# Four weight buffers instead of three, a list that knows what the buffers hold, and a fourth buffer for finished rows

## The chip, the cores and the metric

The kernel runs on one core of a Trainium2 chip. The metric is the device time of one execution in microseconds (us), lower is better. TensorE (PE in the profile) does the matmuls, VectorE (DVE), ScalarE (ACT) and GpSimd (POOL) the rest of the arithmetic, SyncE (SP) issues most DMAs; POOL issues the indirect ones.

## What is computed

There are 14336 tokens of 192 channels. A seven-tap causal filter per head comes first, then two mixtures of experts, each with 8 experts of 192 to 1024 to 192:

```python
x = attn(x, weight)                          # causal filter, taps softmaxed per head
do = x @ w_skip > 0                          # first mixture: only these tokens
e = argmax(x[do] @ w_gate); y = gate * (relu(x @ w1[e]) @ w2[e]); x[do] += y
e2 = argmax(x @ w_gate2 + modality_bias[modality_id])      # second mixture: all tokens
out = gate2 * (relu(x @ w1b[e2]) @ w2b[e2])
```

## The kernel before

Tokens are sorted by expert on the chip and then worked off in blocks ("slots") of 128 rows. A slot is a job: an indirect DMA on POOL gathers the rows (`gather`, tile `gt`), SP transposes them by DMA (`xpose`, tile `xt`, or `xp` for a pair), `mm1` multiplies by the first weight matrix (`w1b`), ACT and DVE split the hidden values into two float16 parts, `mm2` multiplies by the second (`w2b`).

`Ffn.run` writes the 176 jobs out in one fixed order. Jobs 0 to 55 are the first mixture's fixed slots, seven for each expert. Jobs 56 to 61 are its overflow list `l1` (`NS1` = 6 slots for experts with more than 896 tokens). Jobs 62 to 117 are list `lb`: second mixture, the tokens that skipped the first. Jobs 118 to 175 are list `l2`: second mixture, the tokens that the first mixture worked on. In `lb` and `l2` the first 54 and 56 jobs go in pairs that share one set of weights and are multiplied 256 columns at a time; the two last of each list are single.

Which expert a slot belongs to is known only on the chip. `table` writes for each slot the expert and a flag: 1 where this expert differs from the one that last stood in the same buffer. `wload` reads both on SP and issues the load under that flag; a load whose flag is 0 moves nothing. There are three buffers for a pair of weight matrices, taken in turn, so `table` compares with the entry three places earlier (six jobs earlier for pairs); at a list's head it compares with -1, so the first three always load. `wload` is written out as soon as no earlier job still uses the buffer, at most 9 or 10 jobs ahead.

While jobs from 53 on run, `post` takes the first mixture's finished rows in groups of up to four slots: ACT copies them into `h2` (`h` in the profile, three buffers), POOL and DVE complete it, PE and ACT transpose it for the second gate (`xt2`, `xt` in the profile), and SP stores it in `rows2` (line 1153). Three such chains run at a time, handed out in turn by `bg`. ACT, DVE, POOL and PE work strictly in the order written.

The weights of the second mixture are prepared (split in two float16 parts, written to `s1b`, `s2b`) by `lane(1)` in the two tiles `o1` and `o2`, which lie idle after job 53.

Of the kernel before, what the change touches and what calls it, by code (L numbers as in the profile page):

```python
# [12 lines left out]
ALU = mybir.AluOpType  # L13
# [21 lines left out]
XA = 16  # L35
NSEL = 4
LANES = [(0, e) for e in range(E)], [(1, r) for r in range(NSEL)]
RW = 396
# [6 lines left out]
NP2B, NS2B = 27, 56  # L45
NP2A, NS2A = 28, 58
NC1 = NSA + CAP - 1
NR2 = NC1 * 128 + 384
# [67 lines left out]
class Moe:  # L116
# [63 lines left out]

    def plain(self, tmp):
        nc, cp = self.nc, self.cp
        dz = tmp.tile([128, RW], F16, name="rC")
        nc.gpsimd.memset(dz, 0.0)
        nc.gpsimd.memset(f32v(dz.unsqueeze(1))[:, 0, MB + 4:MB + 5], BIGID)
        self.dz = dz
        self.c8 = cp.tile([128, 8], F32, name="c8")
        self.iota(self.c8, [[-1, 8]], base=8)
        self.mt3 = cp.tile([TP, NT, 3], F32, name="mt3")
        nc.gpsimd.memset(self.mt3, 0.0)  # L190
        self.iota(self.mt3[:, :, 1], [[TP, NT]], base=TP - 1, cm=-1)
        self.code = cp.tile([128, 2, NT], F32, name="code")
        nc.gpsimd.memset(self.code, 0.0)
        self.codeA = cp.tile([128, NC1], F32, name="codeA")
        nc.gpsimd.memset(self.codeA, 0.0)
        self.cont = cp.tile([128, 8, GT], F32, name="cont")
        nc.gpsimd.memset(self.cont, 1.0)
        nc.gpsimd.memset(self.cont[:, :, 0:1], 0.0)
        self.iq = cp.tile([128, 128, 8], F16, name="iq")
        self.iota(self.iq, [[1, 128], [0, 8]])  # L200
        self.tri = cp.tile([128, 128], F32, name="tri")
        self.iota(self.tri, [[1, 128]], cm=-1)
        nc.gpsimd.tensor_scalar(self.tri, self.tri, 0.0, None, ALU.is_gt)
        self.val = cp.tile([128, 16], F16, name="val")
        self.iota(self.val, [[1, 16]], base=1, cm=16)
        self.valr = cp.tile([128, 16], F16, name="valr")
        self.iota(self.valr, [[128, 16]], base=1, cm=1)
        self.g2k = cp.tile([128, 9], F32, name="g2k")
        self.iota(self.g2k, [[2048, 9]])

    def tables(self, bias2, wgs, mod, tmp):
        nc, tc, cp = self.nc, self.tc, self.cp
# [43 lines left out]
        nc.gpsimd.tensor_copy(self.modf, mi[:, :, 0])  # L256
        self.bias = cp.tile([TP, NT, 8], F32, name="biasall")
        self.bias_for(nc.gpsimd, self.bias, self.modf, NT, tmp)
# [452 lines left out]

    def table(self, S, np, o, tag, pool, ob, res, lp, top=None):
        nc = self.nc
        en = o[2]
        ef = ob.tile([128, S + 6], F32, name="esl", bufs=1)
        nc.vector.memset(ef[:, 0:6], -1.0)
        for k in range(2 if np else 1):
            ex = pool.tile([128, S, 8], F32, name="rB")
            nc.vector.tensor_tensor(ex, self.iq[:, :S, :], en[:, k].unsqueeze(1).to_broadcast([128, S, 8]), ALU.is_ge)
            yield 1  # L720
            e1 = pool.tile([128, S], F32, name="e1") if k else ef[:, 6:]
            nc.vector.tensor_reduce(e1, ex, AX.X, ALU.add)
            yield 1
        tab = lp.tile([128, S, 2], I32, name="tab" + tag)
        if np:
            nc.vector.tensor_tensor(ef[:, 6:], ef[:, 6:], e1, ALU.add)
            nc.vector.tensor_copy(tab[:, :, 0], ef[:, 6:])
            nc.vector.tensor_scalar(tab[:, :, 0], tab[:, :, 0], 7, None, ALU.bitwise_and)
            nc.vector.tensor_copy(ef[:, 6:], tab[:, :, 0])
        else:  # L730
            nc.vector.tensor_scalar(ef[:, 6:], ef[:, 6:], 7.0, None, ALU.min)
        if top is not None:
            nc.vector.tensor_scalar(ef[:, 6:], ef[:, 6:], float(top), None, ALU.min)
        if top is not None or not np:
            nc.vector.tensor_copy(tab[:, :, 0], ef[:, 6:])
        for a, b, c, d in ((0, 2 * np, 0, 1), (2 * np, min(2 * np + 3, S), 2 * np, 2), (2 * np + 3, S, 2 * np + 6, 1)) if np else ((0, S, 3, 1),):
            if b > a:
                nc.vector.tensor_tensor(tab[:, a:b, 1], ef[:, a + 6:b + 6], ef[:, c:c + d * (b - a - 1) + 1:d], ALU.not_equal)
        res["tab"] = tab
        yield 1  # L740
# [14 lines left out]

    def route(self, code, nst, tag, pool, ob, res, base=0, lag=1, S=None, np=0, lp=None, val=None, perm=False, top=None):
        lp = lp or self.cp
        S = S or nst
        r, o = [], []
        for w in self.ranks(code, pool, 1, r):  # L760
            yield w
        for w in self.slots(r[3], np, perm, pool, o):
            yield w
        self.left(r[3], nst, perm, o, tag, pool, res, lp)
        for w in self.place(r, np, o, pool):
            yield w
        q, sl = self.qsl(o[4], pool)
        yield 1
        for w in self.table(S, np, o, tag, pool, ob, res, lp, top):
            yield w  # L770
        for w in self.invert(S, q, sl, pool, ob, tag, res, lp, lag, base, val):
            yield w
# [229 lines left out]
class Ffn:  # L1002
    def __init__(self, m, ctx, out):
        self.m, self.nc, self.tc, self.out = m, m.nc, m.tc, out
        cp = m.cp
        self.w1b = [cp.tile([128, 4, F], F16, name=f"w1b{i}") for i in range(2)]
        self.w2b = [cp.tile([128, W2C + 2], F16, name=f"w2b{i}") for i in range(2)]
        self.g = ctx.enter_context(m.tc.tile_pool(name="fg", bufs=7))
        self.pairs, self.pw, self.pg = 0, None, None

# [107 lines left out]
    def post(self, x2, mt, nb, va, dst, code):  # L1118
        nc, m, p = self.nc, self.m, self.late
        h2 = p.tile([128, NB1, RW], F16, name="h2", bufs=3)  # L1120
        mo = f32v(h2)[:, :nb, :]
# [55 lines left out]
    def run(self, jobs, bg, pre, fill, need):  # L1177
# [7 lines left out]
        def wload(k, w, m):  # L1185
            if not 0 <= k < n or (k, w) in wl or jobs[k]["s1"] is None or jobs[k]["part"]:
                return
            jb = jobs[k]
            if any(jobs[j]["b"] == jb["b"] for j in range(m, k)):
                return  # L1190
# [109 lines left out]
def build(tc, x, cw, m1w1, m1w2, mod, bias2, m2w1, m2w2, wgs, out):  # L1300
    with ExitStack() as ctx:
# [18 lines left out]
        next(taps)  # L1320
        tables = m.tables(bias2, wgs, mod, rt)
        next(tables)
        for _ in taps:
            pass
        m.consts()
        m.plain(rt)

# [75 lines left out]
        def late_pools():  # L1403
            st.close()
            m.py.append(m.py2)
            m.ph.append(m.ph3)
            px = ctx.enter_context(tc.tile_pool(name="px", bufs=1))
            w["x"] = px.tile([128, NC - XA, D], F32, name="x2s")
            po = sp.enter_context(tc.tile_pool(name="po", bufs=1))
            pw2 = sp.enter_context(tc.tile_pool(name="pw2", bufs=2))  # L1410
            w["pw2"] = pw2
            tkw.add(lane(1))
            o = po.tile([128, 4, F], F16, name="o1"), po.tile([128, W2C + 2], F16, name="o2")
            w["o"] = o
            tk.add(routes())

        def x2of(c, nb):
# [36 lines left out]
        for k in range(NSA - SB + SA, NSA):  # L1454
            jobs[k].update(b=2, s1=s1[0], s2=s2[0], fix=0 if k == NSA - SB + SA else None)
        jobs += [mk(1, l1, j, rows, col=NSA + j, s=0, b=j % 3) for j in range(NS1)]
        for l, nst, np, src, g in ((lb, NS2B, NP2B, rows, NS1), (l2, NS2A, NP2A, rows2, NS1 + NS2B - NP2B)):
            jobs += [mk(2, l, j, src, s=1, b=(g + j // 2) % 3, size=2, part=j % 2) for j in range(2 * np)]
            jobs += [mk(2, l, j, src, s=1, b=(g + j - np) % 3) for j in range(2 * np, nst)]
        n1, n2 = NC, NC + NS2B  # L1460

        def bg(i, pt):
# [9 lines left out]
            if i == n1 - 9 and pt == 4:  # L1472
                tk.drain()
                tkw.drain()
                sp.close()
                ffn.pg = ctx.enter_context(tc.tile_pool(name="pg", bufs=2))
                ffn.pw = pw
                m.ph.pop()
                ffn.late = ctx.enter_context(tc.tile_pool(name="pl", bufs=4))
            if i == n1 - 7 and pt == 0:  # L1480
# [5 lines left out]
            if n1 + 7 < i < n2 - 6 and not tk.live and "idx" not in l2:  # L1486
                tk.add(m.route(m.codeA[:, 0:NC], NS2A, "2", rt, ob, l2, lag=2, np=NP2A, perm=True, top=NSEL - 1))
            if i == n2 and pt == 0:
# [5 lines left out]
            if i == n2 - 6 and pt == 0:  # L1494
                tk.drain()
                if "idx" not in l2:
                    tk.add(m.route(m.codeA[:, 0:NC], NS2A, "2", rt, ob, l2, lag=2, np=NP2A, perm=True, top=NSEL - 1))
                    tk.drain()
# [19 lines left out]
        ffn.rows2 = rows2  # L1518
        ffn.run(jobs, bg, pre, fill, need)
        obr = ctx.enter_context(tc.tile_pool(name="obr", bufs=1))  # L1520
        for n in ("nrem", "un"):
# [61 lines left out]
```

## Time and profile before

| what | value |
|---|---|
| three runs | 1000.71 to 1004.94 us, median 1002.71 |
| profiled execution | 1001.22 us, of which the span from first to last instruction is 999.3 |
| PE busy | 916.0 us, 92% |
| DVE, ACT, POOL busy | 587.8, 476.0, 513.7 us |
| mean granted TensorE clock | 0.968 |
| DMA | 150.79 MB, mean 151 GB/s |

The difference between profiled time and span, 1.9 us, lies outside the first and last instruction. PE's busy share says that it sets the pace; what can be gained is in its idle stretches and in stretches at a lower clock.

### The profile page before, as it was taken

The page shows a single profiled execution, that of the slowest core. Times are in us where ns is not written, and L with a number is a line of the kernel's source. Part 1 is how long each engine was busy: PE and PEld are TensorE (multiplying, and loading weights), DVE is VectorE, ACT ScalarE, POOL GpSimd, SP SyncE. Part 2 cuts the span into 40 slices and gives each one's busy share as a digit, 9 for nine tenths or more (in the row PEclk, how much of TensorE's full clock was granted, in tenths as well). Part 3 has the DMA queues.
Part 4 walks back from the last instruction along what each step waited for, and adds up shares of the span by engine and source line. Part 5 has one row for each costly group of instructions (what it writes and reads, how often), then busy time and mean ns, then how long its engine had stood idle before and what let it go on. Part 6 is the DMA issues. An engine that isn't in the chain of part 4 may idle for free. (4 is left out here: it accounts for less than half of the span.)

```text
span 999.3 us, 28865 instructions
## 1 busy us (share of the span) xinstructions
PE 916.0 (92%) x11000; PEld 852.3 (85%) x11000; DVE 587.8 (59%) x1624; ACT 476.0 (48%) x895; POOL 513.7 (51%) x985
## 2 busy tenths in 40 slices
PE   6999868997999999976999999999989999999993
PEld 4666668987999999976888988999988999999992
DVE  5689977899798877543555465864332333333330
ACT  3877743545686654443645654333333333333430
POOL 4155543742646365562777675454544555555431
PEclk9999859999999999997999999999999999999997
DMA  9595576754868776599333333222492222332240
GB/s 318 192 334 187 186 198 191 197 137 132 237 181 249 214 223 197 163 233 329 91 95 98 109 98 111 70 64 62 135 295 63 73 74 69 74 73 74 74 122 16
DMA packets 106197, 150.79 MB, mean 151 GB/s; under 512 B 80591, under 2 KB 85689, under 8 KB 100800
## 3 DMA queue, kind: packets, MB, share of 16 engines
q1 hardware_dynamic: 91424, 119.34, 38.6%
q0 software_dynamic: 13920, 28.87, 12.1%
q8 instruction: 89, 1.46, 0.6%
q10 hardware_dynamic: 704, 0.63, 0.2%
q14 instruction: 60, 0.49, 0.2%
HBM read 174.22 MB, written 51.08 MB: 225 GB/s over the span
## 5 line engine op out<-in xcount | busy, mean ns | idle before, releaser
L71 PEld LDWEIGHTS <-w1b 128*128 128x128 f16 x4840 | 370.6, 99 | 43.1 <-issue 14.4
L71 DVE SCALAR_TENSOR_TENSOR ws<-bank,ws 128x512 f16<-128x512 f32 x220 | 151.3, 690 | 267.9 <-ACT ws L71 224.4
L71 PE MATMUL bank<-xp,w1b 128*128 128x256 f16 x2200 | 264.6, 274 | 5.2 <-DMA xp<-gt 2.9
L71 PE MATMUL bank<-w2b,ws 128*128 128x192 f16 x2640 | 239.2, 246 | 0.1
L71 PEld LDWEIGHTS <-ws 128*128 128x128 f16 (+2 forms) x2696 | 224.0, 98 | 2.7 <-issue 0.2
L71 POOL DMA_INDIRECT out_dram<-u,si x114 | 115.4, 1012 | 188.0 <-ACT u L71 76.0
L71 ACT ACTIVATE ws<-bank 128x512 f16<-128x512 f32 x220 | 130.6, 597 | 99.5 <-PE bank L71 89.0
L71 PE MATMUL bank<-xt,w1b 128*128 128x128 f16 x2640 | 165.6, 222 | 12.5 <-DVE hlo L71 7.4
L71 ACT ACTIVATE hh<-bank 128x512 f16<-128x512 f32 x132 | 78.5, 594 | 143.6 <-PE bank L71 133.0
L71 PE MATMUL bank<-w2b,hh 128*128 128x192 f16 x1056 | 141.2, 250 | 2.3 <-DMA w2b<-s2a 1.9
L71 PE MATMUL bank<-w2b,hlo 128*128 128x192 f16 x528 | 131.6, 249 | 0.6 <-DVE hlo L71 0.6
L71 ACT ACTIVATE u<-bank,c 128x192 f32<-128x192 f32 x114 | 48.1, 422 | 171.5 <-PE bank L71 148.0
L71 DVE SCALAR_TENSOR_TENSOR hlo<-bank,hh 128x512 f16<-128x512 f32 x132 | 90.0, 685 | 55.2 <-ACT hh L71 49.1
L71 PEld LDWEIGHTS <-hh 128*128 128x128 f16 x1056 | 96.3, 100 | 3.3 <-issue 2.9
L71 POOL DMA_INDIRECT gt<-rows,idxm x62 | 62.7, 1011 | 10.2 <-issue 6.9
L71 POOL TENSOR_TENSOR xs<-gt 128x128 f32<-128x128 f16 x124 | 53.7, 455 | 26.9 <-DVE x2a L71 13.0
L71 POOL DMA_INDIRECT gt<-rows,idx x58 | 57.5, 991 | 9.3 <-issue 6.7
L71 PE MATMUL bank<-xg,band 128*112 128x384 f32 x128 | 57.6, 537 | 1.7 <-DVE hl L71 1.7
L71 ACT COPY xtb<-bank 128x672 f16<-128x672 f16 x64 | 46.0, 720 | 19.2 <-PE bank L71 18.9
L71 PEld LDWEIGHTS <-hlo 128*128 128x128 f16 x528 | 52.4, 99 | 1.0 <-DVE hlo L71 0.8
L71 POOL DMA_INDIRECT gt<-rows,idxs x44 | 47.0, 1069 | 6.7 <-POOL c L71 3.3
L71 POOL TENSOR_SCALAR ef<-ef 128x4 f32<-128x4 f32 (+1 forms) x16 | 4.4, 277 | 86.8 <-DVE ef L71 86.8
(293 smaller groups left out, 1135.1 us busy)
## 6 DMA issues: line engine op xcount, KB each, us to landing
w1b<-s1b SPq DMA_DIRECT2D x59, 1024.0 KB
w2b<-s2b SPq DMA_DIRECT2D x59, 768.5 KB
xg<-in_x_dram SPq DMA_DIRECT2D x7, 1536.0 KB
rows<-hl SPq DMA_DIRECT2D x7, 1386.0 KB
ws<-in_moe_w_dram SPq DMA_DIRECT2D x12, 768.0 KB
s1a<-w1b SPq DMA_DIRECT2D x8, 1024.0 KB
w1b<-s1a SPq DMA_DIRECT2D x7, 1024.0 KB
s2a<-w2b SPq DMA_DIRECT2D x8, 768.5 KB
```

Of the source, the lines that this page charges most:

```text
L71: r = f(*args, **kw)
```

## The change

Overflow slots and second-mixture slots take four buffers in turn, in the order 0, 3, 1, 2. The fourth is made of `o1` and `o2`, whose pool now stays open, and joins the list at job 53. `table` therefore compares four entries back (eight jobs for pairs). For `l2`, the four entries ahead of the list's head are no longer -1 but the experts that the last four weight sets of `lb` left in the buffers (`held`, four copies on DVE). `h2` gets four buffers. To make room, three tables of phase 1 (`mt3`, `cont`, `biasall`) move into a pool that is closed after phase 1, and the pool of the `post` tiles is closed after the last job and made anew with one `h2` buffer for the rarely needed loop behind it. The diff, cut to its core (`ef[:, 6:]` becomes `ef[:, 8:]` throughout `table`; `held` is passed through `route`):

```diff
+RING = (0, 3, 1, 2)
+NR2B = NS2B - NP2B
-        self.mt3 = cp.tile([TP, NT, 3], F32, name="mt3")
+        self.mt3 = st.tile([TP, NT, 3], F32, name="mt3", bufs=1)
-        self.cont = cp.tile([128, 8, GT], F32, name="cont")
+        self.cont = st.tile([128, 8, GT], F32, name="cont", bufs=1)
-        self.bias = cp.tile([TP, NT, 8], F32, name="biasall")
+        self.bias = st.tile([TP, NT, 8], F32, name="biasall", bufs=1)
...
-        ef = ob.tile([128, S + 6], F32, name="esl", bufs=1)
-        nc.vector.memset(ef[:, 0:6], -1.0)
+        ef = ob.tile([128, S + 8], F32, name="esl", bufs=1)
+        nc.vector.memset(ef[:, 0:8], -1.0)
+        for k, v in enumerate(held or ()):
+            nc.vector.tensor_copy(ef[:, 2 * k:2 * k + 1], v)
...
-        h2 = p.tile([128, NB1, RW], F16, name="h2", bufs=3)
+        h2 = p.tile([128, NB1, RW], F16, name="h2", bufs=self.nh)
...
-            if any(jobs[j]["b"] == jb["b"] for j in range(m, k)):
+            if jb["b"] >= len(self.w1b) or any(jobs[j]["b"] == jb["b"] for j in range(m, k)):
...
-            po = sp.enter_context(tc.tile_pool(name="po", bufs=1))
+            po = ctx.enter_context(tc.tile_pool(name="po", bufs=1))
...
+        def held():
+            return [lb["tab"][:, 2 * r if r < NP2B else r + NP2B, 0:1] for r in range(NR2B - 4, NR2B)]
...
-        jobs += [mk(1, l1, j, rows, col=NSA + j, s=0, b=j % 3) for j in range(NS1)]
+        jobs += [mk(1, l1, j, rows, col=NSA + j, s=0, b=RING[j % 4]) for j in range(NS1)]
-            jobs += [mk(2, l, j, src, s=1, b=(g + j // 2) % 3, size=2, part=j % 2) for j in range(2 * np)]
+            jobs += [mk(2, l, j, src, s=1, b=RING[(g + j // 2) % 4], size=2, part=j % 2) for j in range(2 * np)]
...
                 sp.close()
+                ffn.w1b.append(w["o"][0])
+                ffn.w2b.append(w["o"][1])
-                ffn.late = ctx.enter_context(tc.tile_pool(name="pl", bufs=4))
+                ffn.late = sp.enter_context(tc.tile_pool(name="pl", bufs=4))
...
         ffn.run(jobs, bg, pre, fill, need)
+        sp.close()
+        ffn.late, ffn.nh = ctx.enter_context(tc.tile_pool(name="plr", bufs=1)), 1
```

## Rows read from the trace of the kernel before

**Rows 1.** The page, part 2: PE's busy tenths, its clock, GB/s, in 40 slices.
```profile
PE   6999868997999999976999999999989999999993
PEclk9999859999999999997999999999999999999997
...
GB/s 318 192 334 187 186 198 191 197 137 132 237 181 249 214 223 197 163 233 329 91 95 98 109 98 111 70 64 62 135 295 63 73 74 69 74 73 74 74 122 16
```
**Rows 2.** Windows: length, busy PE, PEld, DVE, ACT, POOL (instructions), PEclk, DMA share, GB/s.
```profile
401.00:420.00 19.00, 19.00 (x287) 19.00 (x285) 10.40 (x22) 7.37 (x14) 9.59 (x29) 1.00 0.55 149
...
450.00:460.00 10.00, 7.48 (x80) 6.86 (x80) 2.69 (x8) 1.54 (x3) 0.19 (x1) 0.83 1.09 371
460.00:470.00 10.00, 5.54 (x49) 4.84 (x50) 2.29 (x9) 3.38 (x7) 5.21 (x12) 0.66 0.78 313
```
**Rows 3.** Timeline of PE, 430 to 515: start, length, operation, idle time before it, releaser.
```profile
442.07 1.28 PE L71 MATMUL bank<-xt,w1b 128*128 128x128 f16 x20 [2.11 <-DMA xt<-gt]
...
450.06 1.37 PE L71 MATMUL bank<-xt,w1b 128*128 128x128 f16 x20 [2.38 <-DMA xt<-gt]
...
464.46 0.25 PE L71 MATMUL bank<-g,xt 128*128 128x16 f16 x3 [6.92 <-ACT xt L71]
...
464.83 2.34 PE L71 MATMUL bank<-xp,w1b 128*128 128x256 f16 x10
...
469.77 1.25 PE L71 MATMUL bank<-xp,w1b 128*128 128x256 f16 x10
```
**Rows 4.** Waits of PE, whole span: total us, times, longest.
```profile
PE bank L71 <- DMA w2b<-s2a: 1.9, 2, 1.3
```
**Rows 5.** Timeline of ACT, 425 to 485.
```profile
463.19 0.83 ACT L71 CAST h<-x2a 128x768 f16<-128x768 f32 x1 [8.91 <-DMA rows<-h]
...
474.31 0.83 ACT L71 CAST h<-x2s 128x768 f16<-128x768 f32 x1
```
**Rows 6.** Tile `h`: idle time of its engines before its instructions, times.
```profile
  DMA rows<-h: 12.5, 4
```
**Rows 7.** Timeline of SP's queue, 330 to 500.
```profile
401.21 0.36 SPq L1025 DMA_DIRECT2D w1b<-s1a  x1
...
436.01 1.24 SPq L1031 DMA_TRANSPOSE xt<-gt  x1
...
443.69 1.19 SPq L1031 DMA_TRANSPOSE xt<-gt  x1
...
456.51 0.53 SPq L1153 DMA_DIRECT2D rows<-h  x1
```
**Rows 8.** Timeline of SP's queue, 690 to 770.
```profile
711.04 0.72 SPq L1025 DMA_DIRECT2D w1b<-s1b  x1
...
732.21 0.33 SPq L1025 DMA_DIRECT2D w1b<-s1b  x1
734.13 3.60 SPq L1026 DMA_DIRECT2D w2b<-s2b  x2
739.33 0.08 SPq L1025 DMA_DIRECT2D w1b<-s1b  x1
739.51 2.57 SPq L1031 DMA_TRANSPOSE xp<-gt  x2
```
**Rows 9.** Timeline of PE, 700 to 768.
```profile
750.49 3.52 PE L71 MATMUL bank<-xp,w1b 128*128 128x256 f16 x20 [2.86 <-DMA xp<-gt]
...
756.31 2.35 PE L71 MATMUL bank<-xp,w1b 128*128 128x256 f16 x20
...
760.48 2.35 PE L71 MATMUL bank<-xp,w1b 128*128 128x256 f16 x20
```
**Rows 10.** DMA issues, whole span: times issued, KB each (1024 bytes).
```profile
w1b<-s1b SPq DMA_DIRECT2D x59, 1024.0 KB
w2b<-s2b SPq DMA_DIRECT2D x59, 768.5 KB
```
**Rows 11.** Groups of instructions on DVE by form, 600 to 660: busy us, mean ns.
```profile
L71 DVE TENSOR_REDUCE tt<-se 128x1 f32<-128x8 f32 x2 | 0.3, 160 | 0.1
```

More of the change, by code (lines that the diff above doesn't have):

```diff
@@ L179, in consts, with plain @@
         nc.vector.tensor_copy(self.identf, self.ident)
-    def plain(self, tmp):
+    def plain(self, tmp, st):
         nc, cp = self.nc, self.cp
@@ L209, in plain, with tables @@
         self.iota(self.g2k, [[2048, 9]])
-    def tables(self, bias2, wgs, mod, tmp):
+    def tables(self, bias2, wgs, mod, tmp, st):
         nc, tc, cp = self.nc, self.tc, self.cp
@@ L710, in place, with table @@
         o.append(pos)
-    def table(self, S, np, o, tag, pool, ob, res, lp, top=None):
+    def table(self, S, np, o, tag, pool, ob, res, lp, top=None, held=None):
         nc = self.nc
         en = o[2]
-        ef = ob.tile([128, S + 6], F32, name="esl", bufs=1)
-        nc.vector.memset(ef[:, 0:6], -1.0)
+        ef = ob.tile([128, S + 8], F32, name="esl", bufs=1)
+        nc.vector.memset(ef[:, 0:8], -1.0)
+        for k, v in enumerate(held or ()):
+            nc.vector.tensor_copy(ef[:, 2 * k:2 * k + 1], v)
         for k in range(2 if np else 1):
@@ L720, in table @@
             yield 1
-            e1 = pool.tile([128, S], F32, name="e1") if k else ef[:, 6:]
+            e1 = pool.tile([128, S], F32, name="e1") if k else ef[:, 8:]
             nc.vector.tensor_reduce(e1, ex, AX.X, ALU.add)
@@ L725, in table @@
         if np:
-            nc.vector.tensor_tensor(ef[:, 6:], ef[:, 6:], e1, ALU.add)
-            nc.vector.tensor_copy(tab[:, :, 0], ef[:, 6:])
+            nc.vector.tensor_tensor(ef[:, 8:], ef[:, 8:], e1, ALU.add)
+            nc.vector.tensor_copy(tab[:, :, 0], ef[:, 8:])
             nc.vector.tensor_scalar(tab[:, :, 0], tab[:, :, 0], 7, None, ALU.bitwise_and)
-            nc.vector.tensor_copy(ef[:, 6:], tab[:, :, 0])
+            nc.vector.tensor_copy(ef[:, 8:], tab[:, :, 0])
         else:
-            nc.vector.tensor_scalar(ef[:, 6:], ef[:, 6:], 7.0, None, ALU.min)
+            nc.vector.tensor_scalar(ef[:, 8:], ef[:, 8:], 7.0, None, ALU.min)
         if top is not None:
-            nc.vector.tensor_scalar(ef[:, 6:], ef[:, 6:], float(top), None, ALU.min)
+            nc.vector.tensor_scalar(ef[:, 8:], ef[:, 8:], float(top), None, ALU.min)
         if top is not None or not np:
-            nc.vector.tensor_copy(tab[:, :, 0], ef[:, 6:])
-        for a, b, c, d in ((0, 2 * np, 0, 1), (2 * np, min(2 * np + 3, S), 2 * np, 2), (2 * np + 3, S, 2 * np + 6, 1)) if np else ((0, S, 3, 1),):
+            nc.vector.tensor_copy(tab[:, :, 0], ef[:, 8:])
+        for a, b, c, d in ((0, 2 * np, 0, 1), (2 * np, min(2 * np + 4, S), 2 * np, 2), (2 * np + 4, S, 2 * np + 8, 1)) if np else ((0, S, 4, 1),):
             if b > a:
-                nc.vector.tensor_tensor(tab[:, a:b, 1], ef[:, a + 6:b + 6], ef[:, c:c + d * (b - a - 1) + 1:d], ALU.not_equal)
+                nc.vector.tensor_tensor(tab[:, a:b, 1], ef[:, a + 8:b + 8], ef[:, c:c + d * (b - a - 1) + 1:d], ALU.not_equal)
         res["tab"] = tab
@@ L754, in left, with route @@
             res["un"] = un
-    def route(self, code, nst, tag, pool, ob, res, base=0, lag=1, S=None, np=0, lp=None, val=None, perm=False, top=None):
+    def route(self, code, nst, tag, pool, ob, res, base=0, lag=1, S=None, np=0, lp=None, val=None, perm=False, top=None, held=None):
         lp = lp or self.cp
@@ L768, in route @@
         yield 1
-        for w in self.table(S, np, o, tag, pool, ob, res, lp, top):
+        for w in self.table(S, np, o, tag, pool, ob, res, lp, top, held):
             yield w
@@ L1008, in __init__ @@
         self.g = ctx.enter_context(m.tc.tile_pool(name="fg", bufs=7))
-        self.pairs, self.pw, self.pg = 0, None, None
+        self.pairs, self.pw, self.pg, self.nh = 0, None, None, 4
     def gather(self, idx, src):
@@ L1320, in build @@
         next(taps)
-        tables = m.tables(bias2, wgs, mod, rt)
+        tables = m.tables(bias2, wgs, mod, rt, p1.p2)
         next(tables)
@@ L1325, in build @@
         m.consts()
-        m.plain(rt)
+        m.plain(rt, p1.p2)
         step, scaled = [-1], [0]
@@ L1455, in build @@
             jobs[k].update(b=2, s1=s1[0], s2=s2[0], fix=0 if k == NSA - SB + SA else None)
-        jobs += [mk(1, l1, j, rows, col=NSA + j, s=0, b=j % 3) for j in range(NS1)]
-        for l, nst, np, src, g in ((lb, NS2B, NP2B, rows, NS1), (l2, NS2A, NP2A, rows2, NS1 + NS2B - NP2B)):
-            jobs += [mk(2, l, j, src, s=1, b=(g + j // 2) % 3, size=2, part=j % 2) for j in range(2 * np)]
-            jobs += [mk(2, l, j, src, s=1, b=(g + j - np) % 3) for j in range(2 * np, nst)]
+        jobs += [mk(1, l1, j, rows, col=NSA + j, s=0, b=RING[j % 4]) for j in range(NS1)]
+        for l, nst, np, src, g in ((lb, NS2B, NP2B, rows, NS1), (l2, NS2A, NP2A, rows2, NS1 + NR2B)):
+            jobs += [mk(2, l, j, src, s=1, b=RING[(g + j // 2) % 4], size=2, part=j % 2) for j in range(2 * np)]
+            jobs += [mk(2, l, j, src, s=1, b=RING[(g + j - np) % 4]) for j in range(2 * np, nst)]
         n1, n2 = NC, NC + NS2B
@@ L1486, in bg @@
             if n1 + 7 < i < n2 - 6 and not tk.live and "idx" not in l2:
-                tk.add(m.route(m.codeA[:, 0:NC], NS2A, "2", rt, ob, l2, lag=2, np=NP2A, perm=True, top=NSEL - 1))
+                tk.add(m.route(m.codeA[:, 0:NC], NS2A, "2", rt, ob, l2, lag=2, np=NP2A, perm=True, top=NSEL - 1, held=held()))
             if i == n2 and pt == 0:
@@ L1496, in bg @@
                 if "idx" not in l2:
-                    tk.add(m.route(m.codeA[:, 0:NC], NS2A, "2", rt, ob, l2, lag=2, np=NP2A, perm=True, top=NSEL - 1))
+                    tk.add(m.route(m.codeA[:, 0:NC], NS2A, "2", rt, ob, l2, lag=2, np=NP2A, perm=True, top=NSEL - 1, held=held()))
                     tk.drain()
```

## The prediction

> **What bounds the kernel now.** I read the page's table of slices first. PE is at 9 in nearly every slice, so the end is set by PE, and only PE's holes and its slow stretches can give time back. After phase 1 there are two weak places: the two slices from 450 to 500 us (7 and 6) and the slice from 750 to 775 (8) [rows 1]. A slice is 999.3 / 40 = 25 us.
>
> Then I read the windows around the first place. From 450 to 460 PE is busy 7.48 of 10 us at a granted clock of 0.83, from 460 to 470 only 5.54 of 10 at 0.66, while the DMA engines are busy throughout (shares 1.09 and 0.78, 371 and 313 GB/s) [rows 2]. A DMA burst and a PE hole at the same time: either PE itself waits for data, or something that PE needs waits for the burst.
>
> The timeline of PE names the holes. There is 2.11 us ahead of 442.07 and 2.38 us ahead of 450.06, both ended by the landing of a transposed block, and 6.92 us ahead of 464.46, ended by ACT's copy of a transposed group [rows 3]. The list of waits adds 1.9 us in two waits for `w2b` [rows 4]. Sum: 2.1 + 2.4 + 6.9 + 1.9 = 13.3 us.
>
> The longest hole is not ACT's own work. ACT's timeline shows that it sat 8.91 us ahead of one CAST into `h`, waiting for the store `rows<-h` [rows 5]: the fourth group of finished rows wanted the buffer of the first. ACT works in order, so the copy that PE wanted stood behind that CAST. SP issued the store at 456.51 [rows 7]; the buffer came free at 463.19. The store needed 6.7 us because weights were in flight. The tile view counts four such waits, 12.5 us in all [rows 6].
>
> At the second place, SP's queue shows the weights of list `l2` being loaded: between 711.04 and 732.21 four issues of `w1b` take 0.33 us or longer, where an issue that moves nothing takes about 0.08 [rows 8]. A pair of matrices is 1024 + 768.5 KB [rows 10], 1.84 MB; four are 7.3 MB, which agrees with 295 GB/s in the slice from 725 to 750 against 62 to 74 GB/s in quiet ones [rows 1]. The transposes issued at 739.51 are behind them, and PE waits 2.86 us ahead of 750.49 for a transposed block. The pair step that starts there takes 756.31 - 750.49 = 5.8 us, the next one 760.48 - 756.31 = 4.2 [rows 9].
>
> **The first part: `h2` with four buffers.** It takes away the fourth group's wait for the first group's store. Removed: 6.9 us of PE idle time [rows 3], and the slow stretch behind it. The ten matmuls at 464.83 take 2.34 us, ten like them at 469.77 take 1.25 [rows 3]: 1.1 us lost in these alone; for the window as a whole 5.54 x (1 - 0.66) = 1.9 us [rows 2]. I take 1.7. Sum 8.6 us.
>
> What is late next? The fifth group's CAST, which wants the first group's buffer in the new kernel. It follows the fourth's by 474.31 - 463.19 = 11.1 us [rows 5], of which 1.7 were the clock. Without the wait the fourth runs at about 463.2 - 8.9 = 454.3, the fifth at about 454.3 + 9.4 = 463.7, and the first store lands at 463.2. So it arrives with next to nothing in hand. I take off 1.0 us: 7.6 us stay. Bounds: 8.6 if the store is early, 2.6 if the store lands 6 us later relative to the jobs.
>
> **The second part: four buffers in the overflow list.** A pair of matrices at 371 GB/s [rows 2] takes 1.84 / 0.371 = 4.9 us. A single job has 40 matmuls in `mm1` and 24 in `mm2`; from 401 to 420 PE did 287 in 19 us [rows 2], so 64 take 4.2 us. The six overflow slots and the first three pairs need nine loads in a row, so this stretch runs at the pace of the DMA engines. From 401 to 420 they are only at a share of 0.55 and 149 GB/s [rows 2]: there is room ahead of the burst. With three buffers, the load of overflow slot 2 has to wait for buffer 2, which the first mixture's last four jobs hold until about 401 + 4 x 4.2 = 418. With the order 0, 3, 1, 2 it goes into buffer 1, which is free at 401.21, when slot 1's load went there [rows 7]; slot 1's goes to the new buffer at job 54, about 410. Every later load can start one job earlier, about 4 to 5 us. So one load moves from the burst into the room ahead of it. The two waits for `w2b` (slots 2 and 3) go: 1.9 us [rows 4]. The transposes at 436.01 and 443.69 that PE waited for [rows 7] landed 6 us after their issue; each has one `w1b` and one `w2b` in front of it, and this stays so, one job further on. I count nothing for these 4.5 us, with bounds of +6 us (both waits and their slow stretch go; 10 us at 0.83 [rows 2] are 1.7 us) and -6 us (each gets another pair of matrices ahead of it, less what they have in hand).
>
> List `lb` loads its weights into four buffers instead of three: one load more, 4.9 us of DMA time, behind the others and wanted only three pairs later. From 475 on the engines are far from full (the slices behind are at 91 to 111 GB/s [rows 1]); it costs nothing as long as no transpose stands behind it with less than 4.9 us in hand.
>
> **The third part: `l2` knows what the buffers hold.** Nearly all issues in `lb` and `l2` move nothing [rows 1, 8], so both lists are almost wholly one expert, the most loaded one, and the four issues at 711 to 732 must be one for the last single of `lb` (another expert) and three for the head of `l2`, which compares with -1. With `held`, the first three weight sets of `l2` find that expert in their buffers and move nothing; the fourth finds the single's expert and loads, three pairs later. Four loads become two, 2 x 4.9 = 9.8 us less DMA time around 725 to 745, and the transposes of 739.51 find a free queue. That gives back 2.9 us of waiting and 5.8 - 4.2 = 1.6 us of slow clock [rows 9], and some 0.5 us of small waits around it that I leave out: 4.5 us. The four copies on DVE are of the size of the smallest instructions there, 160 ns [rows 11]: 0.64 us in `l2`'s routing around 640 us, where PE is at 9 in every slice [rows 1]. DVE is nearly full there, so it could cost PE up to 0.6 us; I take 0.3.
>
> The tables that change pools issue nothing new. They are last used in phase 1, and what is laid over them is first written much later. Zero, with a bound of 1 us loss for a write that waits for a last reader.
>
> **Sum.** 7.6 + 1.9 + 0 + 4.5 - 0.3 = 13.7 us. From the profiled execution's 1001.2 us that makes 987.5. The median of the three runs is 1.5 us above this execution, so I expect a median of 989.
>
> **The rivals.** *All holes close.* The transposes of the overflow list land in time as well because the burst starts a load earlier: 6 us more, 983. For it speaks the room at 401 to 420; against it that a load stays in front of each.
>
> *The stall is handed on.* With ACT freed, the fifth group waits for the first store, or PE runs into the burst, since nine loads at 4.9 us are 44 us whatever PE does. Then the first part gives only 2.6 us and the time is 989 + 5 = 994. Against it: the engines fall back to 91 GB/s in the slice from 475 [rows 1], so the burst was over by then, and among PE's waits for weights those for the first mixture's second matrices are the only ones of note, 1.9 us [rows 4].
>
> *Slower: weights in front of transposes.* SP has one queue, and what is behind a load waits for it: the store of 456.51 took 6.7 us, the transposes some 6. Four buffers allow four weight sets in flight, and the order in which SP's instructions are written may put two in front of a transpose where there was one. Each costs PE 4.9 us plus the 1.7 us of slow clock, 6.6 us. Two such stalls use up the gain of 13.7, and from three on, 1002.7 - 13.7 + 19.8 = 1009, the kernel is slower by over 0.5%. The Trainium skill ("DMA: Bandwidth & Descriptors", "Queues, rings and completion order") says that SP owns one ring on each DMA engine, and that a ring is consumed in order; it gives the rule behind this case, and the 6.7 us of the store agree with it. Against the case: the overflow stretch has only six single transposes, and the same count of loads is spread over a longer time.
>
> *It doesn't do what it says.* If the copied entries don't match (another expert, or an order of buffers that is off), `l2` loads four sets instead of three and the second place gets worse by up to 4.9 us: 989 + 4.5 + 4.9 = 998.
>
> **Chances.** The forecast, part by part as above, 0.57 (984.5 to 993); all holes close 0.17; handed on 0.14; slower 0.07; doesn't do what it says 0.05. An effect below 0.5%, 5 us, can't be told from none here. Faster by more (below 997.7): 0.57 + 0.17 + 0.11 of the third case = 0.85. Within: 0.03 of the third, 0.05 of the last and 0.01 of the fourth, where only two stalls come, 0.09. Slower: the other 0.06. The range reaches from 981 (all holes close, with 2 us of the small waits) to 997 (handed on, with nothing left of the first part); below and above it lie about 0.05 and 0.13.
>
> **What would show it.** Right: no wait of ACT for `rows<-h` above 1 us and no PE hole ended by ACT's `xt` at 457; clock 1.00 where it was 0.66; no wait for `w2b<-s2a`; a 1 MB load of `w1b` issued right behind the one at 401; two long issues fewer between 711 and 733; no PE wait at 750. Wrong: new PE waits for `xt<-gt` or `xp<-gt` between 420 and 480, a wait of ACT for `rows<-h` at the fifth group, or PE waiting for weights at the first pairs.

## The result and the profile after

| | before | after |
|---|---|---|
| median, six runs each | 999.57 us | 987.14 us |
| lowest to highest | 994.07 to 1004.94 | 984.29 to 989.52 |
| profiled execution, its span | 1001.22, 999.3 | 987.25, 985.4 |
| PE busy in the span | 916.0 us | 913.1 us |
| DMA | 150.79 MB | 148.96 MB |

The ratio is 0.9875, with a 95% interval of 0.9849 to 0.9902: 12.4 us in the medians, 14.0 in the profiled executions. 989 was forecast, with 981 to 997 as the range; the forecast started from 1002.71, the median of the first three runs, and the six runs of the kernel before have 999.57. DMA fell by 1.83 MB, one pair of matrices: one load more in `lb`, two fewer in `l2`.

The page of the changed kernel, part 2, answers to [rows 1]:

```profile
PE   6999859997999999999899999999999999999993
PEclk9999857999999999999999999999999999999997
...
GB/s 320 207 332 188 188 197 192 177 162 71 299 143 262 200 269 149 244 242 344 140 95 109 98 96 114 72 62 65 144 143 72 72 68 75 74 74 74 71 125 15
```

A slice of the changed kernel is 985.4 / 40 = 24.6 us. The weak place from 425 to 475 (7 and 6 before) is down to one 8 (468 to 493), the 8 from 725 to 750 is gone, and the slice in which `l2`'s weights were loaded moves 143 GB/s instead of 295. The windows of the changed kernel (columns as in [rows 2]) show that the weight burst is as dense as before, and that PE is busy through the middle of it; smaller holes are left at 440 and at 470:

```profile
440.00:450.00 10.00, 7.91 (x104) 7.57 (x102) 3.32 (x13) 3.85 (x9) 7.47 (x22) 0.83 1.02 293
450.00:460.00 10.00, 10.00 (x131) 9.59 (x129) 5.95 (x19) 5.58 (x12) 5.26 (x12) 1.00 1.02 340
460.00:470.00 10.00, 8.64 (x104) 7.88 (x103) 6.70 (x16) 6.92 (x17) 6.36 (x15) 1.00 1.03 407
470.00:480.00 10.00, 7.25 (x69) 6.18 (x68) 5.25 (x25) 3.70 (x8) 2.24 (x8) 0.83 0.79 151
```

PE's timeline at the first place, changed kernel:

```profile
441.72 2.29 PE L73 MATMUL bank<-xt,w1b 128*128 128x128 f16 x20 [1.39 <-DMA xt<-gt]
...
448.82 1.28 PE L73 MATMUL bank<-xt,o 128*128 128x128 f16 x20 [0.70 <-DMA xt<-gt]
...
457.92 1.25 PE L73 MATMUL bank<-xp,w1b 128*128 128x256 f16 x10
...
474.47 1.25 PE L73 MATMUL bank<-xp,w1b 128*128 128x256 f16 x10 [2.75 <-DMA xp<-gt]
...
475.82 2.34 PE L73 MATMUL bank<-xp,w1b 128*128 128x256 f16 x10
...
480.78 1.25 PE L73 MATMUL bank<-xp,w1b 128*128 128x256 f16 x10
```

And two rows of the same view of the kernel before, for the third pair's first and third ten matmuls:

```profile
483.41 1.25 PE L71 MATMUL bank<-xp,w1b 128*128 128x256 f16 x10
...
488.23 1.25 PE L71 MATMUL bank<-xp,w1b 128*128 128x256 f16 x10
```

The ten matmuls that stood at 469.77 [rows 3] are at 457.92: 11.9 us earlier. The two waits for `xt<-gt` went from 2.11 and 2.38 us to 1.39 and 0.70. The third pair starts only 483.41 - 474.47 = 8.9 us earlier, as PE now waits 2.75 us there; behind the wait ten matmuls take 2.34 us, and the pair's third ten come 488.23 - 480.78 = 7.5 us earlier. ACT's timeline says that the buffer wait is gone, for the fourth group's CAST (451.82) and for the fifth's (462.45):

```profile
451.82 0.82 ACT L73 CAST h<-x2a 128x768 f16<-128x768 f32 x1
...
462.45 0.83 ACT L73 CAST h<-x2s 128x768 f16<-128x768 f32 x1
```

SP's queue of the changed kernel has the loads in the order that the new ring gives (`o` is the fourth buffer):

```profile
401.88 0.36 SPq L1029 DMA_DIRECT2D w1b<-s1a  x1
...
410.09 0.33 SPq L1029 DMA_DIRECT2D o<-s1a  x1
...
454.97 0.51 SPq L1157 DMA_DIRECT2D rows<-h  x1
...
458.89 0.34 SPq L1029 DMA_DIRECT2D o<-s1b  x1
...
463.55 0.34 SPq L1030 DMA_DIRECT2D o<-s2b  x1
...
466.10 2.12 SPq L1035 DMA_TRANSPOSE xp<-gt  x2
```

Slot 2's load is where slot 1's was, slot 1's follows at 410. At 458.89 and 463.55 the extra load of `lb` stands in front of the third pair's transposes at 466.10.

At the second place the queue holds two loads instead of four (693.14 with 710.30, and 723.24 with 728.42):

```profile
693.14 0.36 SPq L1029 DMA_DIRECT2D w1b<-s1b  x1
...
710.30 0.37 SPq L1030 DMA_DIRECT2D w2b<-s2b  x1
...
723.24 0.36 SPq L1029 DMA_DIRECT2D w1b<-s1b  x1
...
728.42 0.34 SPq L1030 DMA_DIRECT2D w2b<-s2b  x1
```

PE's timeline there has no wait of note, and the pair steps are 4.2 us where [rows 9] had a hole of 2.86 and a step of 5.8:

```profile
734.32 2.35 PE L73 MATMUL bank<-xp,w1b 128*128 128x256 f16 x20
...
738.49 2.35 PE L73 MATMUL bank<-xp,o 128*128 128x256 f16 x20
...
742.65 2.35 PE L73 MATMUL bank<-xp,o 128*128 128x256 f16 x20
...
746.81 2.35 PE L73 MATMUL bank<-xp,w1b 128*128 128x256 f16 x20
```

The pair half that was at 760.48 [rows 9] is at 746.81, 13.7 us earlier; the first single of `lb` (720.80 before, 711.58 after) was 9.2 us earlier. So the first place, with small steps behind it that were not traced, gave 7.5 to 9.2 us, and the second gave 4.5.

### The profile page after: what moved, and what is told of

The parts are those of the page before. It is cut to its first block, busy times and chain, and to the rows that moved or that the text cites. A ratio compares the mean times of both kernels' runs of the same rounds, so it can differ in the third digit from the quotient of the medians.

```text
span 985.4 us, 28847 instructions
## 1 busy us (share of the span) xinstructions
PE 913.1 (93%) x11000; PEld 851.5 (86%) x11000; DVE 589.1 (60%) x1628; ACT 474.5 (48%) x895; POOL 511.6 (52%) x985
## 2 busy tenths in 40 slices
DMA packets 105910, 148.96 MB, mean 151 GB/s; under 512 B 80559, under 2 KB 85657, under 8 KB 100640
## 5 line engine op out<-in xcount | busy, mean ns | idle before, releaser
L73 PEld LDWEIGHTS <-w1b 128*128 128x128 f16 x4200 | 313.8, 99 | 33.5 <-issue 15.8
L73 PE MATMUL bank<-xp,w1b 128*128 128x256 f16 x1680 | 201.7, 274 | 4.4 <-DMA xp<-gt 2.7
L73 PE MATMUL bank<-w2b,ws 128*128 128x192 f16 x2016 | 182.8, 247 | 0.0
L73 PE MATMUL bank<-xt,w1b 128*128 128x128 f16 x2520 | 159.0, 223 | 9.2 <-DVE hlo L73 7.5
L73 PE MATMUL bank<-w2b,hh 128*128 128x192 f16 x1008 | 134.8, 250 | 0.0
L73 PE MATMUL bank<-w2b,hlo 128*128 128x192 f16 x504 | 126.1, 250 | 0.6 <-DVE hlo L73 0.6
L73 PEld LDWEIGHTS <-o 128*128 128x128 f16 x640 | 57.0, 98 | 7.0 <-issue 1.6
L73 PE MATMUL bank<-xp,o 128*128 128x256 f16 x520 | 62.0, 273 | 0.3 <-issue 0.3
L73 PE MATMUL bank<-o,ws 128*128 128x192 f16 x624 | 56.4, 247 | 0.0
```

What stands on the lines that cost most here:

```text
L73: r = f(*args, **kw)
```

## The experiments

All are timed against the kernel before on the same chip, in three sets. The chips differ by up to 1% (medians of before: 997.8, 990.4 and 990.1 us), so only the ratios are compared across sets. The ratios and intervals are those on record; the quotient of the two medians differs from them by up to 0.002 (0.9958 instead of 0.9978 for ring_three_h2). So a difference of 1 or 2 us between two kernels says nothing.

**1. h2_alone.** The kernel before with

```diff
-        h2 = p.tile([128, NB1, RW], F16, name="h2", bufs=3)
+        h2 = p.tile([128, NB1, RW], F16, name="h2", bufs=4)
```

> Only the fourth h2 buffer is added to the kernel before; three weight buffers and the list heads stay as they were. Theory A (the parts are separate; the store of the first group was the stall): ACT's wait of 8.9 us for rows<-h is gone, PE's hole of 6.9 us and the slow clock behind it with it, 8 to 9 us less than before, ratio 0.991 to 0.992. Theory B (the stall is handed on unless the burst starts a load earlier): the fifth group waits for the first store, or PE for weights, and at most 3 us come back, ratio 0.997 or more.

Measured: 992.19 against 997.8, ratio 0.9935 (0.9912 to 0.9957). Between the two theories, and the trace shows why: ACT's wait is gone, but PE ran into the burst. The fourth group's CAST on ACT, and of PE's list of waits, whole span (the last of them is at the second place, as before):

```profile
452.26 0.82 ACT L71 CAST h<-x2a 128x768 f16<-128x768 f32 x1
...
PE bank L71 <- DMA w1b<-s1b: 4.0, 1, 4.0
...
PE bank L71 <- DMA w2b<-s2a: 3.3, 3, 1.5
...
PE bank L71 <- DMA xp<-gt: 2.1, 1, 2.1
```

and of its timeline:

```profile
459.56 2.31 PE L71 MATMUL bank<-xp,w1b 128*128 128x256 f16 x10 [4.04 <-DMA w1b<-s1b]
...
466.52 1.25 PE L71 MATMUL bank<-xp,w1b 128*128 128x256 f16 x10
```

The first pair's third ten matmuls (466.52) came 3.3 us earlier than in the kernel before (469.77 [rows 3]), not 8.6: the hole of 6.9 us became one of 4.0, with slow matmuls behind it again (2.31 for ten). The rest of the gain in time came in smaller steps later on.

**2. ring_three_h2.** The changed kernel with `self.nh` at 3 instead of 4.

> The changed kernel with three h2 buffers again. Theory A: ACT waits some 8 us for rows<-h at the fourth group and PE loses 8 to 9 us against the changed kernel; 4 to 5 us less than before, ratio 0.995 to 0.997. Theory B (the fourth weight buffer is what counts, as the store comes free sooner): the wait is 3 us or less and the time stays within 3 us of the changed kernel, ratio 0.988 to 0.991.

Measured: 993.62 against 997.8, ratio 0.9978 (0.9957 to 0.9998), nearest to theory A, whose 0.995 to 0.997 lies inside the interval. It is 10.3 us above late_fourth (experiment 4), which is the changed kernel but for one moved load, on the same chip. ACT's and PE's lists of waits, 400 to 520:

```profile
ACT h L73 <- DMA rows<-h: 9.7, 2, 9.4
...
PE bank L73 <- ACT xt L73: 8.9, 2, 8.0
```

The fourth weight buffer does not bring the store home sooner (9.4 us of waiting, 8.9 before).

**3. no_held.** The changed kernel without `held=held()` in the two calls of `route`.

> The changed kernel, but the last list's head compares with -1 again, so that it loads four sets there. Theory A: four sets at its head make the transposes late; the wait of some 3 us and the slow clock come back, 4.5 to 6.5 us above the changed kernel, ratio to before 0.992 to 0.994. Theory B (with four buffers the loads are early enough to be hidden): no wait for xp<-gt at the list's head, same time as the changed kernel, ratio 0.987 to 0.988.

Measured: 991.19 against 997.8, ratio 0.9949 (0.9927 to 0.9971). Theory A: the wait at the head of `l2` is back. It is 7.9 us above late_fourth on the same chip, more than theory A's 4.5 to 6.5.

```profile
739.83 3.43 PE L73 MATMUL bank<-xp,o 128*128 128x256 f16 x20 [3.47 <-DMA xp<-gt]
```

In time it can't be told from h2_alone (0.9935), though it has the fourth weight buffer as well. Its profile is 4.4 us shorter than h2_alone's, the medians differ by 1.0; without `held`, four buffers make `l2` load four sets where three buffers load three. What the fourth weight buffer is worth without `held` stays open.

**4. late_fourth and late_fourth_2.** The changed kernel with the loads of one weight set, the fourth of `lb`, moved behind the third pair's transposes (the expectations say the second pair's, but in the changed kernel these loads, at 458.89 and 463.55, stood behind those already):

```diff
             if "fix" in jb:
...
+            if "hold" in jb and m < jb["hold"][w]:
+                return
...
+        jobs[n1 + 6]["hold"] = (n1 + 4, n1 + 2)
```

> The changed kernel, with one load moved: that of the fourth weight set of the list lb (wanted by its fourth pair) is written behind the second pair's transposes instead of right behind the overflow list. Theory A (the new wait of 2.75 us ahead of 474 is for transposes that stand behind this load): the wait and the slow clock behind it go, 3.5 to 4.5 us less than the changed kernel, ratio to before 0.983 to 0.984. Theory B (the transposes are late for another reason, such as their gathers or the second pair's own loads): the wait stays and the time is that of the changed kernel, 0.987 to 0.988. Theory C (the load is now too late for the fourth pair): PE waits for w1b or w2b ahead of that pair, 2 us or more, and the time is that of the changed kernel or above.

> The changed kernel with the load of the fourth weight set of lb written behind the second pair's transposes, once more beside the changed kernel. Theory A (that load stood in front of the third pair's transposes and cost PE the wait and slow clock): 2.5 to 4 us less than the changed kernel on this chip. Theory B (what the third pair no longer waits is waited elsewhere): within 1 us of it.

Measured: 983.34 against 997.8, ratio 0.9867 (0.9838 to 0.9895); the second time 976.64 against 990.41, ratio 0.9858 (0.9823 to 0.9894). The changed kernel beside it (**after_again**) has 975.35 and 0.9856 (0.9823 to 0.9889).

> The changed kernel once more, on the same chip as the three others, as the measure for them. Every theory: ratio to before 0.986 to 0.990; PE waits 2 to 3 us for xp<-gt ahead of the third pair.

So there is no gain that can be measured. One thing did not come as expected: after_again has no wait for `xp<-gt` ahead of the third pair, but one of 1.94 us that the profile puts down to DVE, and no slow matmuls behind it:

```profile
474.88 1.25 PE L73 MATMUL bank<-xp,w1b 128*128 128x256 f16 x10 [1.94 <-DVE gd L73]
...
476.21 1.25 PE L73 MATMUL bank<-xp,w1b 128*128 128x256 f16 x10
```

The trace of late_fourth_2 does what the edit was for: the third pair starts at 474.36 without a wait, but that is only 0.5 us ahead of after_again. In that same profile PE waited longer earlier on (SP's rows behind PE's):

```profile
445.17 2.29 PE L73 MATMUL bank<-xt,w1b 128*128 128x128 f16 x20 [5.37 <-DMA xt<-gt]
...
474.36 1.25 PE L73 MATMUL bank<-xp,w1b 128*128 128x256 f16 x10
...
465.36 2.59 SPq L1035 DMA_TRANSPOSE xp<-gt  x2
...
468.29 0.90 SPq L1029 DMA_DIRECT2D o<-s1b  x1
```

That wait for the fifth overflow slot's transpose is ahead of the moved load, which SP issues only at 468.29. It was 1.39 us in the changed kernel's profile, 2.14 in after_again's, 4.17 in no_held's, whose code is the same up to there. The lists of waits for `xt<-gt`, 400 to 520, of after_again and no_held:

```profile
PE bank L73 <- DMA xt<-gt: 3.5, 2, 2.1
...
PE bank L73 <- DMA xt<-gt: 5.2, 2, 4.2
```

It varies by more than the moved load is worth. SP's own waits, 425 to 446, in the changed kernel and in late_fourth_2, show a part of it: ahead of that transpose in SP's queue stands one of the first pair, which waits for its gather:

```profile
SPq L1035 <- DMA gt<-rows,idxm: 3.3, 1, 3.3
...
SPq L1035 <- DMA gt<-rows,idxm: 4.7, 1, 4.7
```

Why the gather is waited for longer in one profile than in another stays open; theory A's 2.5 to 4 us did not come.

**5. three_held.** The kernel before with four `h2` buffers and a `held` for three weight buffers:

```diff
+        for k, v in enumerate(held or ()):
+            nc.vector.tensor_copy(ef[:, 2 * k:2 * k + 1], v)
...
+            n = NS2B - NP2B
+            return [lb["tab"][:, 2 * r if r < NP2B else r + NP2B, 0:1] for r in range(n - 3, n)]
```

> The kernel before, with four h2 buffers and with a last list that knows what the three weight buffers hold, but without a fourth weight buffer. Theory A (at the first place both parts are needed, since h2 alone only hands the stall on to the weight burst): PE still waits some 7 to 9 us for w1b<-s1b and w2b<-s2a between 435 and 460, no wait for xp<-gt at the last list's head, 3 to 6 us above the changed kernel, ratio to before 0.991 to 0.993. Theory B (the fourth weight buffer gives back what its extra load costs, so that it is worth nothing): within 1 us of the changed kernel, 0.986 to 0.989.

Measured: 980.82 against 990.41, ratio 0.9901 (0.9867 to 0.9935), 5.5 us above after_again, whose highest run (977.71) is the lowest of this kernel. The waits of PE were of theory A's kind but smaller, 4.1 us for weights instead of 7 to 9, with a longer one for a transpose. It too waits 2.4 us for `xp<-gt` ahead of the third pair, though it has no extra load in `lb`:

```profile
PE bank L71 <- DMA xt<-gt: 3.6, 1, 3.6
...
PE bank L71 <- DMA w2b<-s2a: 2.6, 2, 1.5
...
PE bank L71 <- DMA xp<-gt: 2.4, 1, 2.4
...
PE bank L71 <- DMA w1b<-s1b: 1.5, 1, 1.5
```

**6. early_join.** late_fourth_2 with the fourth buffer joining two jobs earlier:

```diff
-            if i == n1 - 9 and pt == 4:
+            if i == n1 - 11 and pt == 4:
```

> The kernel late_fourth_2 with one number changed: the fourth buffer joins, and the pools change, at job 51 instead of job 53, so that the load of overflow slot 1 can be written two jobs earlier. Theory A (the overflow list is at the pace of the DMA engines, and room ahead of the burst counts): the DMA engines are busier between 400 and 410, the two waits for xt<-gt at 440 to 450 shrink, 1 to 4 us less than late_fourth_2. Theory B (those transposes are late for the order in SP's queue and their gathers, not for bandwidth): the waits stay, same time within 1 us.

Measured: 977.32 against 990.41, ratio 0.9878 (0.9845 to 0.9911): no gain. The load did move (242 GB/s from 400 to 410, 159 in after_again), and one of the waits for `xt<-gt` was still 3.8 us. Its window, columns as before:

```profile
400.00:410.00 10.00, 10.00 (x157) 10.00 (x154) 5.38 (x11) 4.81 (x10) 6.18 (x17) 1.00 0.81 242
```

Theory B: in this profile more room ahead of the burst did not bring these transposes sooner.

**7. act_store_before and act_store_after.** The two kernels with `post`'s store on ACT's queue:

```diff
-        nc.sync.dma_start(dst, mo.bitcast(I32))
+        nc.scalar.dma_start(dst, mo.bitcast(I32))
```

> The kernel before with one edit: post's store into rows2 is issued from ACT's DMA queue instead of SP's. In the trace of before the first group's rows were complete at 446.9, SP issued the store at 456.5, it had landed at 463.2. Theory A (the buffer is held mainly by SP's queue): the store is issued within 2 us of the last write and lands before the fourth group wants the buffer, ACT's wait for rows<-h falls below 2 us, and the time is that of h2_alone, ratio to before 0.992 to 0.996. Theory B (the weight burst keeps any store in flight this long): the wait for rows<-h stays above 5 us, ratio 0.997 or more. Theory C (ACT, which works in order, now waits for the last write itself): new waits of ACT ahead of the store, and no gain.

> The changed kernel with post's store issued from ACT's queue. Theory A (four h2 buffers already hide the store): ratio to before as for the changed kernel, 0.986 to 0.989. Theory B (the store takes SP's time in front of the transposes): PE's wait ahead of the third pair shrinks, 1 to 3 us less, 0.983 to 0.985. Theory C (as above): ACT waits for the last write, slower than the changed kernel by 1 us or more.

Measured: 990.29 against 990.13, ratio 1.000 (0.9977 to 1.0023), and 979.7 against 990.13, ratio 0.9905 (0.9874 to 0.9935). None of the theories for the first holds as it stood. ACT's timeline:

```profile
451.55 0.35 ACTq L71 DMA_DIRECT2D rows<-h  x1
...
457.77 0.83 ACT L71 CAST h<-x2a 128x768 f16<-128x768 f32 x1 [2.51 <-DMA rows<-h]
...
467.51 0.35 ACTq L71 DMA_DIRECT2D rows<-h  x1
...
476.15 0.83 ACT L71 CAST h<-x2s 128x768 f16<-128x768 f32 x1 [5.37 <-DMA rows<-h]
```

and PE's:

```profile
478.38 0.23 PE L71 MATMUL bank<-g,xt 128*128 128x16 f16 x3 [6.00 <-DVE L L71]
```

The store left 1.6 us after the rows were complete (449.9), and the fourth group's wait fell to 2.5 us. But the stores still took about 6 and 8.6 us to land, and so the fifth group waited 5.4, and PE's longest hole, 6.92 us before, is one of 6.00 a group later. The Trainium skill ("DMA: Bandwidth & Descriptors", "Issuing engines are not separate DMA queues") says that DMAs from all issuing engines run on the same 16 DMA engines and interleave; the 6 and 8.6 us from ACT's queue beside the 6.7 us from SP's [rows 5, 7] agree. In the changed kernel the edit brought nothing: its ratio lies above the changed kernel's 0.9875 and 0.9856, though the intervals overlap, so a loss as in theory C is not excluded.

## Why the prediction was right, point by point

**The sum and the two places.** Right: 13.7 us forecast, 14.0 in the profiled executions, 12.4 in the medians. By place, the first was forecast at 7.6 + 1.9 = 9.5 and gave 7.5 to 9.2; the second at 4.5 and gave 4.5. Taken out one at a time, each of the three parts is missed: `h2` by 10.3 us (ring_three_h2), `held` by 7.9 (no_held), the fourth weight buffer by 5.5 (three_held). That the first place's sum came right is in part luck: `h2` was priced too high and the overflow ring too low, as the next paragraphs show, and the two errors nearly cancel.

**The slices.** The prediction reads the weak slices of [rows 1] one place too far: the 7 and the 6 are 425 to 475, the 8 is 725 to 750. Its terms come from windows and timelines, so no sum hangs on it.

**The first part, 7.6 us for `h2`.** Wrong as a price of its own. That ACT is freed was right: the fourth group's CAST, put at about 454.3, ran at 452.26 in h2_alone and 451.82 in the changed kernel. The step that failed is "Removed: 6.9 us of PE idle time" together with the rival's dismissal: the case *the stall is handed on* is what happens when only this part is made. h2_alone gave 0.65%, some 6.5 us (5.6 in the medians), of which only 3.3 show at the first place, as PE met the first pair's weights 4.0 us before they had landed. That the DMA engines fall quiet after 475 had been read as proof that they weren't the limit; h2_alone says that in the kernel before it was the stall itself that gave them time to catch up. The worry about the fifth group, 1.0 us, did not come true with four buffers: its CAST found a free one.

**The second part, 1.9 us for the overflow ring.** Under-sized. Between three_held and after_again, which differ in the fourth weight buffer, lie 5.5 us in the medians (0.45% in the ratios, whose intervals overlap). The mechanism is the one forecast: slot 2's load at 401.88, slot 1's at 410.09, every later one a job earlier. PE waits for no weights at this place in any profile with four weight buffers; with three and four `h2` it waits 4.1 us (three_held) to 7.3 us (h2_alone: 4.0 + 3.3). So its larger service is that it lets the first part's gain through. The two transposes' waits, for which nothing was counted, were 4.5 us before and 2.1 in the changed kernel's profile, but 3.5 in after_again's and 5.2 in no_held's: no gain there stands clear of the scatter. Four `h2` buffers alone gave 0.65%, the fourth weight buffer with `held` but without them 0.22%, all three 1.25 to 1.44%: the parts were priced as if they could be added, and they can't.

**The extra load in `lb`, 0 us.** In the changed kernel's profile it stands in front of the third pair's transposes, PE waits 2.75 us there, and slow matmuls follow; that is one of the prediction's signs of being wrong, and the condition that it named (a transpose behind the load with little in hand). But that the load is the cause is not shown. three_held, which has no such load, waits 2.4 us for the same transposes; after_again, which has it, 1.94 us, put down to DVE; and moving it gave no time.

**The third part, 4.5 us.** Right in kind and size: two loads instead of four, no wait at 750, and no_held brings the wait back (3.47 us). The price of the copies on DVE, 0.3 us, was not measured by itself; nor was the zero for the tables that change pools.

**The rivals.** *It doesn't do what it says* is excluded by the bytes and by the queue. *All holes close* did not come: at the overflow list PE's longest wait for a transpose was 1.4 us in the changed kernel's profile and 2.1 to 5.4 in those of after_again, no_held and late_fourth_2. *Slower* put the store's 6.7 us down to SP's one queue; act_store_before, with about 6 and 8.6 us from ACT's, shows that another queue does not shorten it.

## What to carry to other kernels

Here a stall during a transfer burst also gave the burst time: 8.6 us were read off the trace, and its removal alone gave 3.3 at that place. Before pricing its removal, ask when the data that PE would meet next would have landed, counted from issue at the burst's rate, and not from the trace in which the stall delayed PE. Two parts that relieve the same burst should be priced together. And a list that starts with buffers in a known state should be told of it: comparing with the real content instead of an impossible value was the cheapest part, four instructions for 4.5 us at that place.

## What was unexpected

A 396 KB store took 6 to 9 us to land during the weight burst, from SP's queue as from ACT's (6.7 us in [rows 5, 7], about 6 and 8.6 us in act_store_before), so that an earlier issue moved the wait to the next group and the time stayed at a ratio of 1.000. The wait of the fifth overflow slot for its transpose varied from 1.4 to 4.2 us (with late_fourth_2 to 5.4) between profiles of kernels whose code is the same up to there.
